# Another order of the same operations in a windowed-attention and gated-projection kernel

## The chip, the cores and the metric

The kernel runs on one core of a Trainium2 chip. The metric is the device time of one execution in microseconds; the median of three runs is given, and one further execution was profiled.

## What is computed

Batch 4, 8 heads, 768 positions, head size 64. The attention keeps, for each position, the 4 first positions ("sinks") and a window of 128 positions that ends at it. Its output is the input x of a gated projection with 512 channels.

```python
scores = scale * np.matmul(q, k.transpose(0, 1, 3, 2))
keep = is_sink | in_window
scores = np.where(keep, scores, -1000000000.0)
a = softmax(scores)                       # over the kept positions
x = (a @ v).transpose(0, 2, 1, 3).reshape(B, S, H * D)
for k in range(K):                        # K = 5, causal
    gate_pre += conv_w[k][None, None, :] * xp[:, k:k + S, :]
gate = 1.0 / (1.0 + np.exp(-gate_pre))
val = x @ w_val
return (gate * val @ w_out).astype(np.float32)
```

The weights come as 64-bit floats; the kernel turns each into a high and a low 32-bit part.

## The kernel before

The attention runs in 24 steps, one for a batch, a third of the positions (256) and half of the heads; the names below carry the step's number, as in `tx.7`. Two steps (2m and 2m+1) make one group m of 256 rows and all 512 channels for the projection; there are 12 groups. The whole program is a list of names, ORDER, which the last loop of `banded` walks through: each name calls one function, which issues its instructions there and then. An engine takes its own instructions in the order in which they were issued, and waits by semaphores for the other engines. So ORDER sets the sequence on each of the engines and on the queue that starts the DMAs (SP), and nothing else does.

The names, in the order of the work, with the lines that the profile shows:

- `kq`, `vv`: DMAs of k and q, and of v (with the sink values at the first third). `wvl`, `wol`: DMAs of a quarter of a weight.
- `wva` to `wvf`, `woa` to `wof`: decoding of a quarter of w_val or w_out. a, c, d, f are mostly ScalarE (L140, L159, L154, L186), b is VectorE on integers (L143, L145, L151), c has a GpSimd product (L160), e is four TensorE matmuls (L181 to L183). For two quarters of w_out a variant without TensorE is used, with VectorE (L151 to L168) and GpSimd (L172).
- `s0`, `s1`: scores of half a step, 32 small matmuls (L395), then VectorE masking and maximum (L400, L404 or L409). `e0`, `e1`: the exponentials, eight ScalarE instructions (L420). `rec`, `norm`: reciprocal, and GpSimd scaling (L435 to L443).
- `tx`: 16 transposes of the probabilities on TensorE (L455); `px`, `py`: copies on VectorE (L486) and ScalarE (L494). `sk`: one transpose of the sink probabilities (L463); `ts`: its copy (L471 or L473).
- `vl`: 48 or 32 matmuls with v (L513); `si`: two matmuls with the sink values (L521), which `sv` prepares (L260 on ScalarE, L263 on GpSimd).
- `xc`, `xh`, `hd`: ScalarE copies of the result (L528, L536, L540); `xl`, `c4`: GpSimd (L544, L549); `c0`, `c1`: the convolution on VectorE (L557); `th`: tanh (L562).
- `v0` to `v3`: a quarter of x @ w_val for group m, 12 matmuls of 128 by 128 on 256 columns each (L576), the last four of which read xl; `y`, `g`, `h`, `l`: copy, gate and split of the result (L582, L595, L601, L605).
- `o0` to `o3`: half of one 128-row block of the output product, six matmuls of 128 by 128 on 512 columns (L629); `t0`, `t1`: copy to an osb buffer (L648), `d0`, `d1`: its DMA.
- `fill.n`: n matmuls on zeros (L227), whose result nothing reads.

Two pairs of PSUM banks serve the scores and tx in turn, two single banks serve the projection, the output, sk and the decoding, and one pair serves vl. There are three buffers of k, q and v, four of raw weights, three of osb. Lines of the loop:

```python
    with tc.manual_schedule():
        for n in ORDER.split():
            f, args = events[n]
            f(*args)
```

Of the kernel before, what the change touches and what calls it, by code (L numbers as in the profile page):

```python
# [47 lines left out]
s0.7 l0.1 vl.4 y1.1 g1.1 e0.7 h1.1 l1.1 s1.7 s1.8 o2.1 si.4 e1.7 tx.5 xc.4 xh.4 px.5 hd.4 c4.4 c0.4 c1.4 o3.1
t1.1 o0.1 e1.8 py.5 kq.9 sk.5 ts.5 norm.6 o1.1 t0.1 tx.6 py.6 rec.7 vl.5 si.5 xc.5 xl.4 px.6 c4.5 sk.6 ts.6
hd.5 xh.5 xl.5 s0.9 s0.8 th.4 norm.7 v0.2 v1.2 e0.9 c0.5 tx.7 c1.5 e0.8 rec.8 norm.8 v2.2 py.7 px.7 g0.2 h0.2  # L50
s1.9 kq.10 s1.10 vl.6 l0.2 si.6 xc.6 c4.6 th.5 sk.7 ts.7 hd.6 d0.1 vv.7 v3.2 xh.6 sv.7 o2.2 g1.2 c0.6 o0.2
h1.2 c1.6 e1.9 rec.9 l1.2 o3.2 e1.10 d1.0 t1.2 tx.8 xl.6 px.8 py.8 vl.7 si.7 xc.7 hd.7 xh.7 sk.8 norm.9 ts.8
c4.7 s0.10 tx.9 th.6 px.9 c0.7 d1.11 c1.7 o1.2 t0.2 e0.10 rec.10 xl.7 v0.3 vv.8 py.9 v1.3 vv.9 g0.3 h0.3 kq.12
s0.12 kq.11 s0.11 th.7 d1.2 l0.3 vl.8 si.8 xc.8 hd.8 c4.8 xh.8 d0.2 s1.11 sk.9 e0.11 norm.10 ts.9 xl.8 v2.3
e1.11 v3.3 c0.8 c1.8 g1.3 e0.12 h1.3 o2.3 s1.12 l1.3 kq.13 s1.13 rec.11 e1.12 rec.12 vl.9 si.9 xc.9 th.8 c4.9
hd.9 xh.9 tx.10 px.10 kq.16 py.10 o3.3 t1.3 vv.10 norm.11 o0.3 o1.3 t0.3 c0.9 c1.9 sk.10 ts.10 s0.13 tx.11
py.11 px.11 norm.12 xl.9 vv.13 vl.10 si.10 xc.10 hd.10 xh.10 kq.14 d1.3 tx.12 py.12 px.12 c4.10 c0.10 warm_up
v0.4 xl.10 v1.4 g0.4 d1.1 h0.4 l0.4 vv.11 c1.10 th.9 v2.4 e1.13 v3.4 g1.4 sk.11 ts.11 s1.14 s0.14 h1.4 vl.11
si.11 o0.4 sk.12 ts.12 e0.13 rec.13 l1.4 xc.11 hd.11 c4.11 sv.13 e0.14 norm.13 c0.11 o1.4 kq.18 e1.14 t0.4
c1.11 kq.15 o2.4 d0.3 o3.4 s0.18 s0.15 vv.12 th.11 xh.11 sv.12 vl.12 si.12 t1.4 xc.12 tx.13 rec.14 hd.12 xl.11  # L60
v0.5 c4.12 norm.14 xh.12 e0.15 px.13 c0.12 c1.12 v2.5 xl.12 v3.5 g1.5 py.13 th.10 v1.5 g0.5 h0.5 sk.13 ts.13
s1.15 h1.5 s1.18 d0.4 e1.15 vl.13 l0.5 si.13 o0.5 l1.5 xc.13 rec.15 hd.13 xh.13 s0.16 e0.16 th.12 tx.14 px.14
o2.5 kq.17 o1.5 t0.5 py.14 c4.13 c0.13 o3.5 t1.5 vv.14 e0.18 xl.13 vv.18 c1.13 s1.16 d1.5 sk.14 ts.14 norm.15
sk.15 ts.15 sv.18 vl.14 si.14 xc.14 hd.14 tx.15 px.15 e1.16 c4.14 c0.14 rec.16 py.15 norm.16 e1.18 c1.14 xh.14
v0.6 v1.6 g0.6 v2.6 h0.6 s0.17 vv.15 kq.19 s0.19 vl.15 si.15 rec.18 l0.6 th.13 vv.16 e0.17 xc.15 v3.6 g1.6
xl.14 c4.15 s1.17 hd.15 s1.19 th.14 h1.6 sk.16 ts.16 l1.6 xh.15 c0.15 xl.15 e1.17 rec.17 kq.20 e0.19 o0.6 o1.6
t0.6 tx.16 py.16 c1.15 px.16 v0.7 v1.7 norm.18 sk.18 ts.18 s0.20 d1.4 kq.21 e1.19 d0.6 vl.16 v2.7 e0.20 g0.7
h0.7 norm.17 l0.7 si.16 xc.16 c4.16 hd.16 tx.18 px.18 py.18 tx.17 v3.7 px.17 c0.16 o2.6 o3.6 th.15 g1.7 vv.23
rec.19 xh.16 c1.16 py.17 t1.6 s1.20 h1.7 xl.16 s0.21 e1.20 sk.17 ts.17 norm.19 o0.7 vv.17 th.16 rec.20 d0.5
l1.7 vl.17 si.17 xc.17 c4.17 hd.17 xh.17 e0.21 xl.17 norm.20 d1.6 c0.17 tx.19 py.19 o2.7 o3.7 o1.7 t0.7 c1.17  # L70
th.17 px.19 t1.7 kq.23 d1.7 s1.21 vl.18 d0.7 si.18 xc.18 c4.18 hd.18 vv.19 xh.18 e1.21 sv.19 tx.20 vv.20 px.20
c0.18 v2.8 xl.18 v3.8 g1.8 h1.8 kq.22 c1.18 th.18 v0.8 v1.8 sk.19 py.20 ts.19 g0.8 h0.8 vl.19 si.19 s1.22 l1.8
rec.21 s0.22 xc.19 hd.19 l0.8 xh.19 c4.19 xl.19 sk.20 o0.8 ts.20 o1.8 c0.19 c1.19 norm.21 e1.22 t0.8 d0.8 o2.8
e0.22 rec.22 v0.9 norm.22 th.19 tx.21 px.21 py.21 vl.20 si.20 vv.21 xc.20 c4.20 hd.20 xh.20 xl.20 s1.23 e1.23
s0.23 vv.22 v1.9 g0.9 h0.9 o3.8 t1.8 v2.9 e0.23 v3.9 l0.9 c0.20 c1.20 rec.23 sk.21 norm.23 ts.21 vl.21 si.21
xc.21 c4.21 g1.9 h1.9 l1.9 tx.22 py.22 px.22 tx.23 py.23 hd.21 xh.21 o2.9 xl.21 o0.9 o3.9 c0.21 o1.9 t1.9 t0.9
# [815 lines left out]
```

## Time and profile before

| | |
|---|---|
| median of 3 runs | 263.68 us (263.66 to 263.72) |
| profiled execution | 264.63 us, span 262.8 us |
| mean granted TensorE clock | 0.997 |
| TensorE busy | 253.6 us (97%) |
| VectorE busy | 204.7 us (78%) |
| ScalarE busy | 188.7 us (72%) |
| GpSimd busy | 177.4 us (67%) |

The span runs from the first to the last instruction of the profiled execution. In the rows, PE is TensorE, PEld its weight loads, DVE VectorE, ACT ScalarE, POOL GpSimd, SP the queue of the DMAs. `L513` is line 513 of the kernel; `out<-in` are the program's names for tiles. Matmuls are pipelined, so one's duration overlaps the next; distances are read from start to start.

### The profile page before, as it was taken

Reading aid. Unit: us, or ns where it says so; the run is one execution under the profiler, and the core shown is the slowest. Engines: PE = TensorE matmul, PEld = TensorE weight load, DVE = VectorE, ACT = ScalarE, POOL = GpSimd, SP = SyncE. Lnnn points to the kernel's source line nnn. Section 1 sums busy time; section 2 is a strip of 40 time slices with the busy share of each in tenths; the row PEclk is TensorE's granted clock in tenths of the full one; section 3 lists DMA queues with packets and bytes.
Section 4 is the critical chain, followed back from the end, with each engine's and each line's share of the span. In section 5 each row is a group of like instructions: output and inputs, shape, how many; then the busy total and the mean of one; then the engine's idle time right before and its main releaser. Section 6 shows DMA issues by size and latency. Waiting matters only on the chain.

```text
span 262.8 us, 9921 instructions
## 1 busy us (share of the span) xinstructions
PE 253.6 (97%) x3960; PEld 205.5 (78%) x3964; DVE 204.7 (78%) x561; ACT 188.7 (72%) x692; POOL 177.4 (67%) x241
## 2 busy tenths in 40 slices
...
PEclk9999999999999999999999999999999999999998
...
GB/s 201 379 340 341 113 262 74 109 168 144 106 78 118 183 131 146 218 171 180 63 174 2 161 81 326 78 185 111 142 4 231 68 106 59 2 122 0 2 44 128
DMA packets 27541, 36.45 MB, mean 139 GB/s; under 512 B 2272, under 2 KB 24032, under 8 KB 27488
## 3 DMA queue, kind: packets, MB, share of 16 engines
...
q14 instruction: 20, 0.16, 0.2%
...
## 4 chain that ended last, share of the span: by engine, by line
PE 79%; ACT 9%; POOL 4%; DMA 4%; DVE 1%; issue 1%; POOLq 0%
PE ac L576 24%; PE ac L629 22%; PE xv L513 11%; PE pr L395 9%; PE pr L455 4%; ACT w L420 4%; PE pr L629 3%; PE xv L521 2%; DMA raw<-in_w_val_dram 2%; DMA vs<-in_vsk_dram 2%; POOL xl L544 1%; PE ac L463 1%; POOL gl L605 1%; POOL vh L263 1%; ACT wv_p L140 1%
## 5 line engine op out<-in xcount | busy, mean ns | idle before, releaser
L557 DVE SCALAR_TENSOR_TENSOR sg<-xv,cw,sg 128x256 f32<-128x256 f32 x192 | 77.8, 474 | 3.3 <-POOL sg L549 2.9
L435 POOL TENSOR_TENSOR wx<-w,sm 128x512 f32<-128x512 f32 x48 | 49.2, 1047 | 5.7 <-DVE sm L427 4.0
L420 ACT ACTIVATE w<-pr,ngm 128x132 f32<-128x132 f32 x136 | 48.6, 370 | 1.6
L576 PE MATMUL ac<-xh,wvh 128*128 128x256 f32 x192 | 48.7, 288 | 0.0
L605 POOL TENSOR_TENSOR gl<-sg,gh 128x512 fp32r<-128x512 f32 x24 | 30.8, 1290 | 26.0 <-ACT gh L601 25.8
L576 PE MATMUL ac<-xh,wvl 128*128 128x256 f32 x192 | 47.0, 279 | 0.0
L549 POOL TENSOR_TENSOR sg<-xt,cw 128x512 f32<-128x512 f32 x24 | 25.5, 1063 | 17.9 <-ACT xt L528 16.5
L576 PEld LDWEIGHTS ac<-xh,wvh 128*128 128x128 f32 x192 | 36.2, 189 | 1.7 <-issue 0.5
L576 PEld LDWEIGHTS ac<-xh,wvl 128*128 128x128 f32 x192 | 36.1, 188 | 0.2
L395 PE MATMUL pr<-k,q 64*32 64x168 f32 x1536 | 35.0, 307 | 0.6 <-DVE wt L486 0.2
L513 PEld LDWEIGHTS xv<-wt,v 64*64 64x64 f32 x1024 | 30.3, 133 | 6.1 <-issue 2.6
L513 PE MATMUL xv<-wt,v 64*64 64x192 f32 (+2 forms) x1024 | 34.5, 278 | 0.2 <-ACT wt L494 0.2
L544 POOL TENSOR_TENSOR xl<-xt,xh 128x512 fp32r<-128x512 f32 x24 | 31.0, 1290 | 3.9 <-DVE sm L427 2.5
L629 PE MATMUL ac<-woh,gh 128*128 128x512 f32 x80 | 33.2, 415 | 0.0
L629 PE MATMUL ac<-woh,gl 128*128 128x512 f32 x80 | 31.8, 397 | 0.3 <-POOL gl L605 0.3
L629 PE MATMUL ac<-wol,gh 128*128 128x512 f32 x80 | 31.7, 396 | 0.0
L576 PE MATMUL ac<-xl,wvh 128*128 128x256 f32 x192 | 30.4, 280 | 0.1
L395 PEld LDWEIGHTS pr<-k,q 64*32 64x32 f32 x1536 | 24.0, 106 | 8.1 <-issue 2.1
L400 DVE COPY_PREDICATED pr<-low,pr 128x256 f32<-128x256 uint8 x48 | 20.3, 422 | 9.6 <-PE pr L395 4.9
L420 ACT ACTIVATION_READ_ACCUMULATOR w<-pr,ngm 128x1 f32 x136 | 27.6, 203 | 0.0
L576 PEld LDWEIGHTS ac<-xl,wvh 128*128 128x128 f32 x192 | 25.9, 188 | 0.3 <-POOL xl L544 0.3
L404 DVE TENSOR_REDUCE ngm<-pr 128x4 f32<-128x528 f32 x34 | 24.0, 707 | 1.2
...
## 6 DMA issues: line engine op xcount, KB each, us to landing
...
q<-in_qt_dram SPq DMA_DIRECT2D x23, 256.0 KB, 4.6
out_dram<-osb SPq DMA_DIRECT2D x23, 256.0 KB, 2.5
v<-in_vt_dram SPq DMA_DIRECT2D x8, 256.0 KB, 5.0
...
```

Of the source, the lines that this page charges most:

```text
L395: nc.tensor.matmul(ss[e * QB:(e + 1) * QB, j, c * n + x0:c * n + x1], q[js, g, (4 * c + e) * QB:(4 * c + e + 1) * QB], k[js, g, (2 * c + e ...
L400: nc.vector.copy_predicated(sv[:, :, :, :D], low[:, None, None, :].to_broadcast([P, 2, 2, D]), sv[:, :, :, 2 * HB:])
L404: nc.vector.tensor_reduce(out=ngm[:, g], in_=sv[:, :, :, :PK], axis=mybir.AxisListType.X, op=ALU.max)
L420: nc.scalar.activation(out=w[:, g, j, c], in_=sx[:, j, c, :PK], func=AF.Exp, scale=0.125 if whole else -1.0, bias=ngm[:, g, j, c:c + 1], a ...
L435: nc.gpsimd.tensor_tensor(out=t[:, n].rearrange("p c h x -> p h c x"), in0=w[:, :, :, at], in1=sm.to_broadcast([P, 4, 2, D]), op=ALU.mult)
L513: nc.tensor.matmul(acc[o * D:(o + 1) * D, g, x0 + h * D:x0 + (h + a1 - a0 + 1) * D], v[js, g, n], t[js, n % 2, n // 2, g, a0:a1 + 1].rearr ...
L544: nc.gpsimd.tensor_tensor(out=half(xls, s, "xl", F32R), in0=xts[s], in1=half(xhs, s, "xh", F32R).bitcast(F32), op=ALU.subtract)
L549: nc.gpsimd.tensor_tensor(out=half(sg, s, "sg", F32), in0=xts[s], op=ALU.mult, in1=cw[:, g, KT - 1:].to_broadcast([P, 2, PQ]))
L557: nc.vector.scalar_tensor_tensor(out=g, in0=x, scalar=a, in1=g, op0=ALU.mult, op1=ALU.add)
L576: nc.tensor.matmul(acc[:, h], a[:, kc, cs], x[:, kc], start=(n == 0), stop=(n == 11))
L605: nc.gpsimd.tensor_tensor(out=gl, in0=g, in1=gh.bitcast(F32), op=ALU.subtract)
L629: nc.tensor.matmul(acc, a[:, kc, ts], x[:, kc], start=(kc + n == 0), stop=(kc + n == 5))
```

## The change

ORDER is replaced by another sequence of the same 849 names; no function changes. The first lines and some later ones of both:

```diff
--- before.py
+++ after.py
@@ -34,50 +34,50 @@
 ORDER = """
-masks load_conv wvl.0 signs kq.0 leads conv_weights fill.5 wva.0 wvb.0 wvd.0 s0.0 wvl.1 s1.0 wvc.0 wve.0 wvl.2
-wva.1 kq.1 wvb.1 e0.0 blanks wva.2 wvb.2 vv.0 e1.0 wvf.0 fill.10 s1.1 wvc.2 wvc.1 rec.0 norm.0 wvd.1 e1.1 s0.1
-fill.4 fill.7 kq.2 s1.2 wol.0 woa.0 wve.1 sv.0 e0.1 e1.2 wob.0 woc.0 wol.2 tx.0 fill.6 px.0 sk.0 py.0 rec.1
-ts.0 wod.0 s0.2 vl.0 woe.0 wvl.3 wva.3 norm.1 wvb.3 kq.3 e0.2 s0.3 wof.0 wvf.1 si.0 xc.0 tx.1 px.1 fill.6 c4.0
-kq.5 wvc.3 rec.2 norm.2 xh.0 wvd.2 hd.0 c0.0 wvd.3 e0.3 wve.2 c1.0 py.1 wol.3 wol.1 woa.1 wve.3 vv.1 wob.1
-wvf.3 sv.1 tx.2 py.2 px.2 s1.3 xl.0 sk.1 ts.1 wod.1 wvf.2 kq.4 vl.1 si.1 xc.1 c4.1 sk.2 ts.2 kq.6 hd.1 woc.1
-s0.4 xh.1 vv.2 woe.1 c0.1 e1.3 rec.3 woa.3 th.0 vv.5 e0.4 xl.1 v0.0 v1.0 c1.1 y0.0 wob.3 woa.2 norm.3 g0.0
-wod.3 h0.0 vl.2 wob.2 th.1 s1.4 e1.4 l0.0 v2.0 v3.0 woe.3 woe.2 y1.0 g1.0 vv.6 tx.3 px.3 si.2 xc.2 hd.2 wof.1
-h1.0 s0.6 o2.0 o0.0 rec.4 xh.2 py.3 c4.2 c0.2 l1.0 wof.2 s0.5 c1.2 s1.6 kq.7 wod.2 e0.6 wof.3 o1.0 t0.0 o3.0
-norm.4 sk.3 e0.5 vv.3 ts.3 t1.0 xl.2 vl.3 si.3 xh.3 xc.3 hd.3 xl.3 c4.3 sk.4 th.2 s1.5 ts.4 tx.4 sv.6 px.4
-e1.5 kq.8 c0.3 scalars d0.0 py.4 rec.5 v0.1 v1.1 y0.1 c1.3 e1.6 rec.6 v2.1 norm.5 g0.1 th.3 h0.1 v3.1 vv.4
...
-o1.10 l1.11 o1.11 t0.10 d0.10 t0.11 o3.10 t1.10 o2.11 d1.10 d0.11 o3.11 t1.11
+masks load_conv d1.11 fill.6 wvl.0 kq.0 signs leads conv_weights wva.0 wvl.2 wvb.0 s0.0 wvc.0 wvd.0 wva.2 e0.0
+s1.0 kq.1 wvb.2 wve.0 wvl.1 e1.0 fill.5 s1.1 wva.1 blanks wvb.1 wvc.2 rec.0 fill.4 norm.0 fill.6 e1.1 kq.2
+wvc.1 wvf.0 wol.0 wvl.3 s0.1 s1.2 e0.1 wvd.1 fill.10 rec.1 woa.0 tx.0 px.0 sk.0 vv.0 wve.1 e1.2 wob.0 wol.3
+s0.2 py.0 wva.3 norm.1 vl.0 kq.3 tx.1 woc.0 wod.0 ts.0 px.1 woe.0 wvb.3 vv.1 sv.0 si.0 e0.2 wvf.1 xc.0 xh.0
+vv.2 hd.0 s0.3 c4.0 rec.2 fill.7 norm.2 wvd.2 py.1 c0.0 wof.0 woa.3 c1.0 wve.2 wob.3 kq.4 sv.1 e0.3 tx.2 sk.1
+py.2 xl.0 kq.6 px.2 ts.1 woe.3 vl.1 sk.2 si.1 s1.3 s1.4 wvc.3 wol.1 ts.2 xc.1 xh.1 wvd.3 hd.1 wve.3 xl.1 wvf.2
+c4.1 woa.1 wvf.3 wob.1 v0.0 e1.3 c0.1 c1.1 wol.2 v1.0 wod.1 wof.3 woa.2 th.0 v2.0 kq.5 woc.1 v3.0 rec.3 y0.0
+vv.3 g0.0 s0.4 woe.1 wob.2 e1.4 s1.6 th.1 y1.0 e0.4 h0.0 vl.2 vv.6 wof.1 g1.0 woe.2 norm.3 vv.5 si.2 xc.2 xh.2
+s0.6 l0.0 kq.7 c4.2 wof.2 s0.5 sk.3 ts.3 h1.0 wod.2 wod.3 l1.0 o2.0 o0.0 tx.3 hd.2 sv.6 o3.0 c0.2 e0.6 px.3
+c1.2 rec.4 xl.2 norm.4 o1.0 e0.5 py.3 s1.7 e1.6 th.2 s0.7 vl.3 t0.0 si.3 d0.0 s1.5 tx.4 t1.0 xh.3 xc.3 hd.3
+vv.4 kq.8 e0.7 px.4 xl.3 sk.4 ts.4 c4.3 v0.1 d1.0 c0.3 v1.1 v2.1 rec.6 e1.5 rec.5 py.4 kq.15 c1.3 v3.1 y0.1
...
+px.5 norm.6 rec.7 xh.4 c0.4 xl.4 ts.5 py.5 o2.1 e1.8 kq.9 c1.4 s0.8 tx.6 norm.7 vl.5 si.5 t0.1 sk.6 py.6 px.6
+e0.8 xh.5 o3.1 kq.10 rec.8 ts.6 xc.5 hd.5 xl.5 scalars s1.9 t1.1 c4.5 norm.8 vv.7 s0.9 e1.9 sk.7 ts.7 c0.5
+v0.2 sv.7 th.4 v1.2 c1.5 v2.2 v3.2 tx.7 e0.9 g0.2 th.5 h0.2 py.7 tx.8 g1.2 l0.2 vl.6 h1.2 si.6 px.7 rec.9 px.8
...
+o0.11 g1.11 o1.10 h1.11 l1.11 o1.11 t0.10 o3.10 t0.11 d0.10 d0.11 o2.11 t1.10 o3.11 d1.10 t1.11
 """
 SKA = 6
```

`d1.11` stands for nothing in either list: the last block is sent by `o3.11` and `t1.11` themselves.

## Rows read from the trace of the kernel before

**Rows 1.** The page's slices: the granted TensorE clock in 40 equal slices of the span, in tenths of full speed.

```profile
PEclk9999999999999999999999999999999999999998
```

**Rows 2.** Busy time by stretches: the stretch and its length in us, then for each engine its busy us and (x instructions), the granted clock, the DMA share and GB/s.

```profile
30.00:40.00 10.00, 8.72 (x139) 6.03 (x138) 9.74 (x23) 9.94 (x36) 9.30 (x12) 1.00 0.57 178
40.00:50.00 10.00, 10.00 (x174) 8.62 (x173) 9.82 (x19) 9.04 (x32) 6.20 (x8) 1.00 0.38 114
50.00:60.00 10.00, 10.00 (x190) 7.68 (x190) 8.06 (x31) 8.29 (x33) 8.68 (x11) 1.00 0.51 137
...
38.20:200.00 161.80, 161.67 (x2787) 136.44 (x2786) 137.02 (x383) 126.11 (x485) 117.35 (x152) 1.00 0.44 134
```

**Rows 3.** TensorE's instructions in order of time, from five places of the trace: start us, duration us, engine, line, operation, out<-in, shape, count.

```profile
46.31 0.71 PE L455 MATMUL pr<-ident,wx 64*128 64x64 f32 x16
46.83 0.36 PE L521 MATMUL xv<-skt,vh 64*128 64x256 f32 x2
...
87.09 0.38 PE L521 MATMUL xv<-skt,vh 64*128 64x256 f32 x2
87.41 0.33 PE L463 MATMUL ac<-ident,skb 128*128 128x128 f32 x1
87.49 0.36 PE L576 MATMUL ac<-xh,wvh 128*128 128x256 f32 x1
...
95.63 0.80 PE L395 MATMUL pr<-k,q 64*32 64x168 f32 x32
96.36 0.71 PE L455 MATMUL pr<-ident,wx 64*128 64x64 f32 x16
...
190.22 0.39 PE L521 MATMUL xv<-skt,vh 64*128 64x256 f32 x2
190.45 0.66 PE L455 MATMUL pr<-ident,wx 64*128 64x64 f32 x16
191.03 0.50 PE L629 MATMUL ac<-woh,gh 128*128 128x512 f32 x1
...
203.82 0.27 PE L463 MATMUL ac<-ident,skb 128*128 128x128 f32 x1
204.03 1.21 PE L513 MATMUL xv<-wt,v 64*64 64x192 f32 x32
```

**Rows 4.** The same view for the first 40 us; in brackets the idle time before an instruction and what ended it.

```profile
10.45 0.50 PE L183 MATMUL ac<-wv_f,plus 128*128 128x512 f32 x1 [0.85 <-POOL wv_f L160]
...
13.06 1.37 PE L395 MATMUL pr<-k,q 64*32 64x168 f32 x64
14.36 2.55 PE L227 MATMUL ac<-zero 128*128 128x512 bf16 x10
...
17.57 1.13 PE L181 MATMUL ac<-wv_t,ident 128*128 128x512 f32 x2
...
19.09 0.71 PE L455 MATMUL pr<-ident,wx 64*128 64x64 f32 x16
...
38.21 0.28 PE L576 MATMUL ac<-xh,wvh 128*128 128x256 f32 x1
```

**Rows 5.** The chain of work that ended last, in order of time: start us, us that the piece adds to the chain (overlap with the next taken off), what.

```profile
19.70 1.52 ACT w L420 x8
...
22.87 0.52 ACT woh L154
...
27.06 0.55 ACT wv_p L159
...
31.48 0.57 ACT wo_p L140
32.05 0.49 ACT wvl L186
...
58.85 5.80 PE ac L576 x48
```

**Rows 6.** ScalarE's instructions in order of time, the copy xh.1.

```profile
36.27 0.68 ACT L536 ACTIVATE xh<-xv 128x512 fp32r<-128x512 f32 x1
```

**Rows 7.** TensorE's instructions in order of time at v0.2 and v1.2, and at o0.8.

```profile
80.05 1.03 PE L576 MATMUL ac<-xl,wvh 128*128 128x256 f32 x4
...
81.85 0.62 PE L576 MATMUL ac<-xl,wvh 128*128 128x256 f32 x4
...
207.36 0.40 PE L629 MATMUL ac<-wol,gh 128*128 128x512 f32 x1
208.04 0.50 PE L629 MATMUL ac<-woh,gl 128*128 128x512 f32 x1 [0.28 <-POOL gl L605]
```

**Rows 8.** Groups of instructions by line over the whole span: line, engine, operation, out<-in, shapes, count | busy us, mean ns of one | idle us before them and what ended it.

```profile
L544 POOL TENSOR_TENSOR xl<-xt,xh 128x512 fp32r<-128x512 f32 x24 | 31.0, 1290 | 3.9 <-DVE sm L427 2.5 <-ACT xt L528 1.2
...
L528 ACT ACTIVATE xt<-xv 128x512 f32<-128x512 f32 x24 | 14.4, 600 | 10.8 <-PE xv L521 10.8
```

**Rows 9.** All instructions of line 143: count, then duration in ns as minimum, median and maximum, first and last start us.

```profile
L143 DVE TENSOR_SCALAR wv_t<-wv_p x4: 420/518/814, 6.7 to 24.7; 128x512 int32<-128x512 int32 x4
L143 DVE TENSOR_SCALAR wo_t<-wo_p x4: 427/530/967, 18.8 to 42.7; 128x512 int32<-128x512 int32 x4
```

**Rows 10.** The same for line 227, the matmuls on zeros.

```profile
L227 PE MATMUL ac<-zero x34: 379/379/634, 3.7 to 27.6; 128*128 128x512 bf16 x34
```

**Rows 11.** DMA issues of one kind: queue, count, KB each, median us from issue to landing.

```profile
out_dram<-osb SPq DMA_DIRECT2D x23, 256.0 KB, 2.5
```

More of the change, by code (lines that the diff above doesn't have):

```diff
@@ L47 @@
-e1.5 kq.8 c0.3 scalars d0.0 py.4 rec.5 v0.1 v1.1 y0.1 c1.3 e1.6 rec.6 v2.1 norm.5 g0.1 th.3 h0.1 v3.1 vv.4
[L48 to L76, printed above, removed]
@@ L77 @@
-c1.21 px.23 th.20 sk.22 ts.22 vl.22 si.22 xc.22 c4.22 xh.22 xl.22 sk.23 ts.23 d1.9 hd.22 c0.22 c1.22 v0.10
-v2.10 v1.10 th.22 g0.10 v3.10 h0.10 l0.10 vl.23 si.23 xc.23 c4.23 hd.23 xh.23 xl.23 th.21 flag g1.10 o0.10
-o2.10 d1.8 c0.23 c1.23 v0.11 v1.11 th.23 g0.11 h0.11 l0.11 v2.11 d0.9 v3.11 g1.11 o0.11 h1.10 l1.10 h1.11
-o1.10 l1.11 o1.11 t0.10 d0.10 t0.11 o3.10 t1.10 o2.11 d1.10 d0.11 o3.11 t1.11
+masks load_conv d1.11 fill.6 wvl.0 kq.0 signs leads conv_weights wva.0 wvl.2 wvb.0 s0.0 wvc.0 wvd.0 wva.2 e0.0
@@ new lines @@
+e1.7 vl.4 th.3 y1.1 g0.1 h0.1 norm.5 g1.1 s1.8 h1.1 tx.5 si.4 xc.4 hd.4 l0.1 sk.5 vv.8 l1.1 c4.4 o0.1 o1.1
+px.5 norm.6 rec.7 xh.4 c0.4 xl.4 ts.5 py.5 o2.1 e1.8 kq.9 c1.4 s0.8 tx.6 norm.7 vl.5 si.5 t0.1 sk.6 py.6 px.6
+e0.8 xh.5 o3.1 kq.10 rec.8 ts.6 xc.5 hd.5 xl.5 scalars s1.9 t1.1 c4.5 norm.8 vv.7 s0.9 e1.9 sk.7 ts.7 c0.5
+v0.2 sv.7 th.4 v1.2 c1.5 v2.2 v3.2 tx.7 e0.9 g0.2 th.5 h0.2 py.7 tx.8 g1.2 l0.2 vl.6 h1.2 si.6 px.7 rec.9 px.8
+xc.6 kq.12 xh.6 s1.10 l1.2 py.8 c4.6 o0.2 norm.9 hd.6 vv.12 c0.6 e1.10 s0.10 o2.2 o3.2 c1.6 e0.10 s0.12 vl.7
@@ new lines @@
+d0.1 si.7 tx.9 rec.10 t1.2 xc.7 xh.7 xl.6 c4.7 px.9 hd.7 e0.12 xl.7 s1.12 o1.2 t0.2 e1.12 py.9 c0.7 kq.11 c1.7
+th.6 v0.3 sk.8 th.7 ts.8 v1.3 g0.3 norm.10 s1.11 h0.3 s0.11 l0.3 d1.2 vl.8 si.8 sk.9 xc.8 hd.8 v2.3 xh.8 c4.8
+ts.9 e1.11 o0.3 c0.8 c1.8 kq.13 vv.9 v3.3 g1.3 xl.8 s0.13 e0.11 h1.3 th.8 s1.13 vl.9 tx.10 si.9 xc.9 sk.10
+ts.10 l1.3 rec.11 o1.3 xh.9 kq.18 hd.9 c4.9 e0.13 px.10 e1.13 c0.9 d1.1 vv.10 c1.9 o2.3 o3.3 norm.11 py.10
+s0.18 s1.18 vl.10 tx.11 rec.12 t0.3 si.10 sk.11 t1.3 xl.9 ts.11 hd.10 v2.4 py.11 xc.10 xh.10 d1.3 th.9 c4.10
@@ new lines @@
+norm.12 v0.4 px.11 kq.14 c0.10 v3.4 v1.4 vv.11 vv.13 c1.10 g0.4 sv.12 tx.12 g1.4 vl.11 e0.18 si.11 py.12 px.12
+d0.3 h0.4 s0.14 h1.4 s1.14 xc.11 l0.4 hd.11 d0.2 vv.14 sk.12 l1.4 o2.4 ts.12 rec.13 e1.14 c4.11 o3.4 o0.4
+c0.11 e0.14 c1.11 o1.4 norm.13 tx.13 xh.11 kq.19 px.13 rec.14 t1.4 t0.4 py.13 kq.16 vl.12 si.12 xl.10 s1.15
+xc.12 s0.15 xl.11 th.10 hd.12 sk.13 c4.12 ts.13 vv.16 v2.5 sv.13 xh.12 v3.5 c0.12 th.11 g1.5 e1.15 norm.14
+e0.15 e1.18 v0.5 tx.14 c1.12 h1.5 sk.14 v1.5 px.14 l1.5 py.14 g0.5 vl.13 h0.5 ts.14 si.13 l0.5 hd.13 rec.15
```

17 lines of the change are left out of this document (added).

## The prediction, made before the changed kernel was run

> **What bounds the kernel now.** I read the slices of the page first, then the busy time by stretches, then TensorE's instructions in order of time, then ScalarE's through the first 40 us. The granted clock stands at full speed in every slice but the last [rows 1]. From 40 us on TensorE is busy in whole stretches, while the other engines leave room [rows 2]. So behind 40 us the time is the sum of TensorE's blocks, and an order can change it in two ways only: by what a block costs behind its neighbour, and by waits. In front of 40 us it is different: ScalarE is busy 9.94 of 10 us, TensorE only 8.72 [rows 2], and part of that is work on zeros. There the order of ScalarE's queue sets when the first projection, v0.0, can start: it starts at 38.21 us [rows 4].
>
> **What a block costs depends on its neighbour.** Read the distances from start to start in [rows 3]. The sink transpose (sk, L463) takes 0.08 us (87.41 to 87.49) ahead of a 128-by-128 matmul, but 0.21 us (203.82 to 204.03) ahead of the small attention matmuls of L513. The sink product (si, L521) takes 0.32 us ahead of anything (87.09 to 87.41) but a probability transpose (tx, L455): there it is 0.23 (190.22 to 190.45). A tx takes 0.58 ahead of a wide matmul (190.45 to 191.03), 0.52 ahead of si (46.31 to 46.83).
>
> **The change part by part.** Every name of the old order is in the new one, as often: 849 names, 38 zero matmuls, the same DMAs. So nothing is removed or added; the sum has three terms.
>
> *Neighbours.* Counted in the two lists, with every name that issues no matmul left out:
>
> - sk stands ahead of val or out 8 times now and 19 times then; ahead of scores, values, si, decode 15 and 5 times (once ahead of another sk before). At 0.08 and 0.21 that is 8 x 0.08 + 15 x 0.21 + 0.17 (an estimate for the one between the two) = 3.96 against 19 x 0.08 + 5 x 0.21 = 2.57: -1.4 us. At the dearest price, 0.25, which I get if scores behind it cost more than values, -1.9.
> - si ahead of tx 10 and 2 times: eight lose 0.09 each, +0.7 us.
> - tx ahead of si or another tx 3 and 12 times. At 0.52 and 0.58 to 0.60 that is -0.5 to -0.7 us; for tx ahead of sk (4 times, none before) I have no row and take the wide price. tx ahead of tx has no row here either; I price it as tx ahead of si. I take -0.6; the ends are 0 (the saving belongs to what stands ahead of tx) and -1.0.
> - val and out stand ahead of attention blocks 23 and 27 times. A score block of 32 ends 0.73 behind its start (95.63 to 96.36), 0.65 each when two follow each other (13.06 to 14.36) [rows 3, 4], so a change of shape costs about 0.1: +0.2 us at most 0.4.
>
> Sum: -1.4 + 0.7 - 0.6 + 0.2 = -1.1 us, ends -0.3 and -1.9.
>
> The Trainium skill, "TensorE: Matmul & The Clock Gate", section "Back-to-back issue gap", gives the distance of two matmuls from the columns alone, with no term for the neighbour; by it this term would be 0. The rows of sk, 0.08 against 0.21 for the same instruction, disagree with it; the case is a rival below.
>
> *The start.* Ahead of xh.1, the ScalarE copy that closes the first group's input, the new queue no longer holds wvd.3, woa.1, wvf.3, wod.1, wvf.2, woc.1; it holds woa.3 in addition. By the net steps of the chain, L154 0.52, L140 0.57, L186 0.49, L159 0.55 [rows 5], that is 2 x 0.52 + 0.57 + 2 x 0.49 + 0.55 - 0.57 = 2.6 us less. xh.1 ended at 36.95 [rows 6], so it would end near 34.4. Two things eat some of it. sv.0 on GpSimd now stands behind woc.0, so si.0, and with it ScalarE's xc.0, comes some 0.4 us later (one L160 against sv's pieces, an estimate from the engine order); behind xc.0 wait xh.0 and wvd.2, and for that wve.2. And wvd.3 now follows xh.1 (+0.5) and wve.3, the last decode ahead of v0.0, needs it for its last two matmul groups: half of the 1.52 us that an undisturbed decode takes (17.57 to 19.09 [rows 4]) plus a little, 0.9. So v0.0 starts near 34.4 + 0.4 + 0.5 + 0.9 = 36.2 instead of 38.2: 2.0 us earlier. But TensorE work was moved behind it: s0.4 (0.73) and woe.1 (1.52) now follow v0.0, s1.4 (0.57 as the second of two scores) precedes it: 1.7 us. Net -0.3 us. Bounds: -1.2 (GpSimd holds nothing up) and +0.8 (the DVE queue, which now has wob.3 and woe.3 ahead of s1.3, comes last).
>
> DMAs: kq.1 now goes out ahead of wvl.1, vv.0 behind wol.0 and wvl.3 on SP's queue. ScalarE reaches wva.1 after e1.0, and vl.0 stands behind 16 us of TensorE work, so I cost both at nothing; what covers them is ScalarE's backlog. If vv.0 came last, vl.0 would wait, at most the length of one 512 KB load. The sends (d) move as well: there are three osb buffers, and t1.5 now needs d0.5 to have landed, which stands some 3 us of TensorE work ahead of it; a send lands 2.5 us behind its issue [rows 11]. Covered, but barely; without that cover ScalarE would stand still for a few tenths, with py and exps behind it.
>
> *Waits behind 40 us.* Two of the old order's waits are large enough to see [rows 7]: the four xl matmuls of v0.2 take 1.03 us instead of 0.62 (0.4), and the third matmul of o0.8 starts 0.68 behind the second instead of 0.23 (0.45, for gl on GpSimd). In the new list the TensorE work between si.5 and v0.2 is doubled (two val blocks' worth instead of one), and between the val blocks of group 8 and o0.8 it grows by some 1 us, so both should go: -0.85. One comes: between si.3 and v0.1 only s1.5, tx.4 and sk.4 are left, 1.3 us, and the xl matmuls come some 0.9 later (eight matmuls); against this stand two copies of 0.60 and one xl of 1.29 [rows 8]: +0.3, by which all of TensorE's queue behind v0.1 moves. I take -0.3, not -0.55, since a new order has waits that a count doesn't show; ends -0.85 and +1.5.
>
> *VectorE's integer operations.* L143 takes 0.42 us at best and up to 0.81 and 0.97 [rows 9]. All eight at the minimum would give VectorE about 1 us (medians 0.52 and 0.53, two far above). In the start ScalarE is the full engine, so I cost it at nothing; ends -0.4 and +0.4, since the new list moves these instructions among as much GpSimd work.
>
> The end: the last six blocks, from o0.11 to o3.11, stand in the same sequence in both lists, so the tail stays.
>
> Sum: -1.1 - 0.3 - 0.3 = -1.7 us. The profiled execution took 264.63 us (262.8 of it span), the median of the runs is 263.68; I carry the difference over: span near 261.1, profiled execution 262.9, median **262.0 us**. For this kernel 0.2% (0.53 us) is what a measurement can tell from no change.
>
> **Rivals.**
>
> *A. The neighbours' prices don't add up.* If a saved gap is only moved into the next block, the first term is about 0 and 0.6 us are left: 263.1. For it: tx's price differs by what stands ahead of it. Against: sk's two prices. This is also the case in which the change doesn't do what its words say: the clock is at full speed already, and VectorE is not what the start waits for. Chance 0.20.
>
> *B. ScalarE becomes the bound from v0.0 to v0.1 (slower).* In the old order this stretch holds 4 exps and 25 other ScalarE entries, in the new one 7 and 27. At 1.52 us an exp [rows 5] that is 4.6 us, with the two others 5.6, on top of the 17.3 us ScalarE was busy between 40 and 60 us [rows 2]: 22.9. TensorE gains s0.4, woe.1, s0.7 and s1.7 and loses s1.4, about 2.7 us on the 20.6 us from 38.21 to 58.85 [rows 4, 5]: 23.3. So ScalarE has 0.4 us to spare; if it also waits as long as before (2.7 us in those 20), v0.1 comes 2.3 us late and nothing behind it has idle time to give it back: 263.68 - 1.7 + 2.3 = 264.3. It decides once the lateness exceeds 2.2 us. Against: part of that work (e0.7, ts.4) isn't needed for v0.1. Chance 0.13.
>
> *C. TensorE's clock drops in the start (slower).* The new order opens with fill.6 instead of fill.5, and later has fill.5, then fill.4 and fill.6, then fill.10 where the old one had fill.10 early. A zero matmul takes 0.63 us while the clock is low and 0.38 when it is not [rows 10]. If waits between fill.5 and fill.10 let it fall to 1.2 GHz for some 5 us of TensorE work that nothing covers, that is +2.5 to +3: 264.7. The Trainium skill, "TensorE: Matmul & The Clock Gate", section "HAM oscillation — how this bites in real kernels", says that waiting TensorE falls back to half clock and starts the next work cold; it speaks against thinner cover. The trace agrees only in that the clock held through waits of 0.85 us [rows 4]. Chance 0.05.
>
> *D. Both engine queues fit better than counted.* The start gives its -1.2 and the waits their -0.85: 263.68 - 1.1 - 1.2 - 0.85 = 260.5. Chance 0.12.
>
> **How the numbers follow.** The forecast's own case (261.3 to 262.9) has 0.50, A 0.20, D 0.12, B 0.13, C 0.05. Faster by over 0.2% (below 263.15): the forecast, D and a third of A, 0.68. Within: the rest of A and a little of B, 0.17. Slower: the rest of B, and C, 0.15. The range runs from D to between A and B's far side: 260.4 to 264.3; the likeliest case alone 261.3 to 262.9.
>
> **What would show it.** v0.0 starting near 36.2 us; sk mostly 0.08 us from its successor; TensorE's busy sum near 252; no 1.03 us xl group at v0.2; the granted clock full in all slices but the last. Wrong if v0.1 starts more than 1 us later than 59.0 us with ScalarE full before it, if idle time of TensorE behind 40 us grows beyond 2 us, or if a slice of the first ten shows a lower clock.

## The result: 1.4% slower, and where the time went

The changed kernel takes **267.27 us** (median of four runs, 267.25 to 267.32) against 263.70 for the kernel before in the same session (263.66 to 263.76): ratio 1.0136, 95% interval 1.0118 to 1.0153. The forecast was 262.0, the range ended at 264.3; both are wrong, and so is the sign. The profiled execution of the new kernel took 267.28 us, its span 265.5.

The page of the new kernel, TensorE's and the other engines' busy time and the slices of the granted clock:

```profile
PE 253.2 (95%) x3961; PEld 204.8 (77%) x3964; DVE 210.2 (79%) x561; ACT 188.1 (71%) x692; POOL 177.8 (67%) x241
PEclk9999999999999999999999999999999999999999
```

The clock is full in every slice (a 9 stands for 90% or more; the mean granted clock is 1.000), so rival C is out. TensorE is busy about as long as before (253.6 us there). The busy time that moved most is VectorE's: 204.7 us before, 210.2 now, for the same 561 instructions. The stretches that answer to [rows 2]:

```profile
30.00:40.00 10.00, 9.27 (x147) 6.91 (x146) 9.90 (x17) 8.06 (x27) 9.60 (x12) 1.00 0.37 104
40.00:50.00 10.00, 8.66 (x176) 6.47 (x175) 9.72 (x23) 9.52 (x37) 6.11 (x8) 1.00 0.13 43
50.00:60.00 10.00, 8.68 (x121) 5.96 (x121) 9.90 (x30) 8.04 (x31) 7.30 (x7) 1.00 0.35 109
```

From 40 to 60 us TensorE is no longer busy throughout (8.66 and 8.68 of 10), ScalarE has some room (9.52 and 8.04), and VectorE (the third pair) is close to full in all three stretches. TensorE's instructions at the two places that the prediction named, v0.0 and v0.1, and below them v0.1 before:

```profile
37.23 0.28 PE L576 MATMUL ac<-xh,wvh 128*128 128x256 f32 x1
...
64.38 0.36 PE L576 MATMUL ac<-xh,wvh 128*128 128x256 f32 x1
```

```profile
58.78 0.39 PE L576 MATMUL ac<-xh,wvh 128*128 128x256 f32 x1
```

v0.0 comes 1.0 us earlier than before [rows 4], v0.1 5.6 us later. To split this into work and waiting I gave each block of TensorE's list the start-to-start distance that its kind has ahead of its successor's kind in the trace of before, and summed these down each list. What a block starts later than that sum is waiting, counted from the start of the span:

| | sum of blocks | waited by v0.0 | by v0.1 | by the last block |
|---|---|---|---|---|
| before | 243.80 | 8.04 | 8.59 | 12.88 |
| after | 242.61 | 8.72 | 13.15 | 16.59 |

So the neighbours gave 1.19 us, the start lost 0.68, the stretch from v0.0 to v0.1 lost 3.9 (4.44 against 0.55), and behind v0.1 the new order gained 0.85 (3.44 against 4.29): together +2.5, for spans that differ by 2.7. How the total splits hangs on the distance that stands for a pair. With the least, the lower quarter or the median of each pair the stretch loses 3.9 to 4.1 us and the start 0.7 to 0.9; the neighbours give 1.2 to 2.2, and the part behind v0.1 gains 0.3 to 0.9. The loss in the stretch is firm, the two gains are less so.

**What holds that stretch.** The shares of the engines in the whole chain of work that ended last, before and then now:

```profile
PE 79%; ACT 9%; POOL 4%; DMA 4%; DVE 1%; issue 1%; POOLq 0%
```

```profile
PE 79%; DVE 15%; issue 2%; POOL 1%; ACT 1%; DVEq 0%; POOLq 0%
```

VectorE had 1% of it and has 15%. Pieces of the new chain, in order of time, from 34 us to v0.1 (start, us that the piece adds, what):

```profile
34.94 0.77 DVE wo_e L151
35.71 1.43 DVE wo_f L166
37.16 1.66 DVE wo_p L168
...
47.46 1.12 DVE wo_t L143
...
51.66 1.19 DVE wo_e L151
...
64.62 1.41 PE ac L576 x12
```

VectorE's integer operations are not more, they are longer. Instructions of their lines in the new kernel (count, ns as minimum, median, maximum, first and last start):

```profile
L143 DVE TENSOR_SCALAR wo_t<-wo_p x4: 416/792/1189, 20.8 to 47.4; 128x512 int32<-128x512 int32 x4
...
L145 DVE SCALAR_TENSOR_TENSOR wv_t<-wv_p,wv_t x4: 691/693/1641, 6.8 to 27.0; 128x512 int32<-128x512 int32 x4
L145 DVE SCALAR_TENSOR_TENSOR wo_t<-wo_p,wo_t x4: 693/760/1412, 22.0 to 48.6; 128x512 int32<-128x512 int32 x4
...
L166 DVE TENSOR_SCALAR wo_f<-raw x2: 419/957/1495, 35.6 to 52.8; 128x512 int32<-128x512 int32 x2
...
L168 DVE SCALAR_TENSOR_TENSOR wo_p<-raw,wo_f x2: 695/1180/1664, 37.2 to 53.2; 128x512 f32<-128x512 uint32 x2
```

The same view of before, for L145 and L166:

```profile
L145 DVE SCALAR_TENSOR_TENSOR wv_t<-wv_p,wv_t x4: 691/692/693, 7.1 to 25.5; 128x512 int32<-128x512 int32 x4
L145 DVE SCALAR_TENSOR_TENSOR wo_t<-wo_p,wo_t x4: 691/692/693, 19.5 to 43.3; 128x512 int32<-128x512 int32 x4
...
L166 DVE TENSOR_SCALAR wo_f<-raw x2: 415/418/420, 45.3 to 46.7; 128x512 int32<-128x512 int32 x2
```

Over all 28 of these instructions (L143, L145, L151, L166, L168 of eight decodes), what they take above their lines' minima is 6.9 us now and 1.6 before; the difference, 5.3, is nearly all of VectorE's growth of 5.5. And what they meet shows in the order of time, VectorE first, then GpSimd:

```profile
35.63 1.50 DVE L166 TENSOR_SCALAR wo_f<-raw 128x512 int32<-128x512 int32 x1
37.16 1.66 DVE L168 SCALAR_TENSOR_TENSOR wo_p<-raw,wo_f 128x512 f32<-128x512 uint32 x1
...
35.37 1.47 POOL L160 TENSOR_TENSOR wv_f<-wv_e,wv_p 128x512 fp32r<-128x512 f32 x1
36.80 1.48 POOL L544 TENSOR_TENSOR xl<-xt,xh 128x512 fp32r<-128x512 f32 x1
38.23 1.50 POOL L549 TENSOR_TENSOR sg<-xt,cw 128x512 f32<-128x512 f32 x1
```

L166 starts inside L160 and ends 0.29 us behind it; L168 starts inside L544 and ends 0.5 behind that. GpSimd pays too: L160 takes 1.47 where it took 1.28 before, L549 1.50 where its median is 1.05. By the trace, 11 of the 28 now overlap a GpSimd instruction of 0.9 us or more for over 0.05 us (called a meeting here), and carry 6.5 of the 6.9 us; before it was 5 with 1.1. So the new order has more of these meetings than the old one, not as many.

How they reach TensorE shows in what ended the idle time before an instruction (in brackets), first TensorE, then ScalarE:

```profile
25.24 1.13 PE L181 MATMUL ac<-wo_t,ident 128*128 128x512 f32 x2 [1.00 <-ACT skt L471]
...
44.99 1.12 PE L181 MATMUL ac<-wo_t,ident 128*128 128x512 f32 x2 [1.23 <-ACT vc L582]
...
39.94 0.20 ACT L417 ACTIVATE ngm<-ngm 128x4 f32<-128x4 f32 x1 [1.91 <-DVE ngm L404]
```

These are the two longest waits of TensorE between 14 us and v0.1; no wait of TensorE names a DMA. The engines in the brackets are ScalarE, but ScalarE itself had stood still for VectorE: 0.82 us for the L145 at 22.0 us, which with the L143 ahead of it took 1.5 us more than their minima, and 1.91 us for the L404 that came behind the L166 and L168 above.

### The profile page after: what moved, and what is told of

It is laid out like the page before. It is cut to its first block, busy times and chain, and to the rows that moved or that the text cites. A ratio compares the mean times of both kernels' runs of the same rounds, so it can differ in the third digit from the quotient of the medians.

```text
span 265.5 us, 9964 instructions
## 1 busy us (share of the span) xinstructions
PE 253.2 (95%) x3961; PEld 204.8 (77%) x3964; DVE 210.2 (79%) x561; ACT 188.1 (71%) x692; POOL 177.8 (67%) x241
## 4 chain that ended last, share of the span: by engine, by line
PE 79%; DVE 15%; issue 2%; POOL 1%; ACT 1%; DVEq 0%; POOLq 0%
PE ac L576 24%; PE ac L629 20%; PE xv L513 10%; PE pr L395 9%; PE pr L455 5%; DVE sg L557 3%; PE pr L629 3%; PE xv L521 2%; PE ac L463 2%; DVE sx L409 2%; DVE pr L400 1%; PE ac L227 1%; PE ac L181 1%; DVE wo_t L143 1%; DVE wt L486 1%
## 5 line engine op out<-in xcount | busy, mean ns | idle before, releaser
L557 DVE SCALAR_TENSOR_TENSOR sg<-xv,cw,sg 128x256 f32<-128x256 f32 x192 | 77.7, 474 | 10.2 <-POOL sg L549 7.0
L549 POOL TENSOR_TENSOR sg<-xt,cw 128x512 f32<-128x512 f32 x24 | 26.0, 1084 | 23.6 <-ACT xt L528 23.4
L576 PEld LDWEIGHTS ac<-xh,wvl 128*128 128x128 f32 x192 | 36.2, 188 | 0.3
L544 POOL TENSOR_TENSOR xl<-xt,xh 128x512 fp32r<-128x512 f32 x24 | 31.1, 1300 | 5.9 <-ACT xh L536 5.4
L404 DVE TENSOR_REDUCE ngm<-pr 128x4 f32<-128x528 f32 x34 | 24.1, 708 | 1.2
```

The source lines that it names most:

```text
L404: nc.vector.tensor_reduce(out=ngm[:, g], in_=sv[:, :, :, :PK], axis=mybir.AxisListType.X, op=ALU.max)
L544: nc.gpsimd.tensor_tensor(out=half(xls, s, "xl", F32R), in0=xts[s], in1=half(xhs, s, "xh", F32R).bitcast(F32), op=ALU.subtract)
L549: nc.gpsimd.tensor_tensor(out=half(sg, s, "sg", F32), in0=xts[s], op=ALU.mult, in1=cw[:, g, KT - 1:].to_broadcast([P, 2, PQ]))
L557: nc.vector.scalar_tensor_tensor(out=g, in0=x, scalar=a, in1=g, op0=ALU.mult, op1=ALU.add)
L576: nc.tensor.matmul(acc[:, h], a[:, kc, cs], x[:, kc], start=(n == 0), stop=(n == 11))
```

## The experiments

Theory 1: the new order loses 4 us because in its start VectorE's decode instructions and GpSimd's long ones hold each other up, and it gains behind v0.1 as forecast. Rivals: the sequence of VectorE's queue itself (more of other work ahead of what TensorE needs), waits of the new order in general, and gaps that don't add up. The kernel before stood at 263.97 us beside the first four kernels, 263.99 beside the second four, 263.80 and 264.21 beside the last two pairs. With the waiting counted as above:

| kernel | us | sum of blocks | by v0.0 | by v0.1 | by the last block |
|---|---|---|---|---|---|
| e3_new_plain | 264.49 | 242.61 | 7.87 | 10.32 | 13.76 |
| e4_old_plain | 265.77 | 243.80 | 8.36 | 10.10 | 14.11 |
| e7_new_two | 265.17 | 242.61 | 7.33 | 10.95 | 14.38 |
| e8_new_one | 266.92 | 242.61 | 9.36 | 13.14 | 16.53 |
| e5_old_start_cut | 263.78 | 242.75 | 7.55 | 9.12 | 12.67 |
| e11_old_to_64 | 263.46 | 242.85 | 8.01 | 8.57 | 12.86 |

**The meeting taken away, in both orders.**

```diff
-        nc.vector.tensor_scalar(out=t, in0=p, scalar1=3, op0=ALU.logical_shift_left, ...)
-        nc.vector.scalar_tensor_tensor(out=t, in0=p, scalar=-2147483648, in1=t, ...)
+        plain(tf, pf)
+        plain(tf, pf)
...
+    def plain(o, x):
+        nc.vector.tensor_reduce(out=o, in_=x[..., None], axis=mybir.AxisListType.X, op=ALU.max)
```

> The new order, with the five integer instructions of each weight decode on VectorE (L143, L145, L151, L166, L168) replaced by reductions over an axis of length one: same tiles, same count, one SBUF input, about 0.6 us each by the nearest row; the weights' low parts are therefore not the real ones. Theory 1 (what VectorE lost it lost because these instructions and GpSimd's hold each other up): each takes its 0.6 us however GpSimd stands, v0.1 starts 2 us or more earlier than 64.4, and the time is 263 to 265 us, at most 1 us above the same edit on the old order. Rival (it is the sequence of VectorE's queue itself, more decode work ahead of the scores' and the convolution's entries): 266.5 us or more, 3 us above the same edit on the old order.

> The same replacement in the old order (the weights' low parts are not the real ones). Theory 1 and its rival alike: VectorE was not what the old start waited for, so 263.2 to 264.4 us; it is the base against which the new order with this edit is read.

Measured: 264.49 us for the new order (ratio to before 1.0021, 1.0009 to 1.0032), 265.77 for the old (1.0065, 1.0044 to 1.0087). With the same edit the new order is 1.3 us *faster* than the old, where the unedited one is 3.6 slower. The first expectation held. The second missed: the old order pays 1.8 us for the edit, by which eighteen of its 28 instructions became 0.26 us longer, so VectorE did stand in the old start's way. The replaced instructions of the new order (line 143 is here the reduction):

```profile
L143 DVE TENSOR_REDUCE wv_t<-wv_p x8: 674/686/686, 6.3 to 25.9; 128x512 f32<-128x512 f32 x8
...
L143 DVE TENSOR_REDUCE wo_t<-wo_p x8: 674/686/687, 20.5 to 45.7; 128x512 f32<-128x512 f32 x8
L143 DVE TENSOR_REDUCE wv_e<-wv_t x4: 686/686/687, 7.7 to 26.7; 128x512 f32<-128x512 f32 x4
```

None of them is held (0.67 to 0.69 us), at the same places in the same queue among the same GpSimd work, though 16 of the 28 meet an instruction of it. TensorE's two waits of 1.00 and 1.23 us are gone, and v0.0 starts at 36.39 us. Waiting by v0.1 is 10.32 us against 10.10 in the old order: of the 4.6 us by which the new order was behind there, 0.2 are left. In the stretch from v0.0 to v0.1 alone it is 0.7 of 3.9, and the start makes up the rest; one VectorE instruction that the edit leaves alone, L595, is still held there, 1.66 us against 0.96 in the old order. The rival, the sequence of VectorE's queue, would have kept its 3 us; it falls.

**One form at a time, in the new order.**

```diff
 # e7: L145 and L168 (two SBUF tiles), L145 below      e8: L143, L151 and L166 (one SBUF tile), likewise
-        nc.vector.scalar_tensor_tensor(out=t, in0=p, scalar=-2147483648, in1=t, ...)
+        nc.vector.tensor_reduce(out=tf, in_=pf[..., None], axis=mybir.AxisListType.X, op=ALU.max)
```

> The new order, with only the two decode instructions that read two SBUF tiles (L145, L168) replaced by a reduction over an axis of length one, 0.68 us each, as long as the two undisturbed (0.69); the weights' low parts are not the real ones. L143, L151, L166 stay. If both forms are held by GpSimd: the ten replaced ones lose their 2.8 us of lengthening and the eighteen others keep about their 4.0, so 265.5 to 266.7 us. If only the pairs of the two reading two tiles matter: 264.5 or less. If this form doesn't matter: 267 or more.

> The new order, with only the decode instructions that read one SBUF tile (L143, L151, L166; 0.42 us undisturbed) replaced by the same reduction at 0.68 us; the weights' low parts are not the real ones. L145 and L168 stay. VectorE gets eighteen times 0.26 us more to do (4.7) and loses the 4.0 us by which these are lengthened: if both forms are held, 266 to 267.3 us, and the traces show L145 and L168 between 0.69 and 1.7 us, the reductions all near 0.68. If the one-input form is not held by GpSimd but only queued, the time grows by the added work, to 268.5 or more.

Measured: 265.17 us (1.0049, 1.0034 to 1.0065) and 266.92 (1.0115, 1.0096 to 1.0134). The first lies 0.3 below the range expected for "both forms are held" and 0.7 above the one for "only the pairs of the two", the second inside the range for "both". What stayed is held in either, first the one-input form of the first kernel, then the two-input form of the second:

```profile
L143 DVE TENSOR_SCALAR wo_t<-wo_p x4: 414/1092/1190, 20.0 to 45.3; 128x512 int32<-128x512 int32 x4
...
L166 DVE TENSOR_SCALAR wo_f<-raw x2: 414/960/1507, 34.0 to 50.7; 128x512 int32<-128x512 int32 x2
```

```profile
L145 DVE SCALAR_TENSOR_TENSOR wv_t<-wv_p,wv_t x4: 693/695/1396, 7.4 to 27.0; 128x512 int32<-128x512 int32 x4
...
L168 DVE SCALAR_TENSOR_TENSOR wo_p<-raw,wo_f x2: 692/1222/1751, 36.9 to 53.2; 128x512 f32<-128x512 uint32 x2
```

**The orders spliced at v0.1.**

```diff
 # e1: old list up to py.4 rec.5, then what is left in the new list's sequence:
 py.4 rec.5 d1.11 s1.7 e1.6 s0.7 vv.4 e0.7 v0.1 d1.0 v1.1 v2.1 rec.6 ...
 # e2: new list up to v0.1, then what is left in the old list's sequence
 e1.5 c0.3 scalars py.4 rec.5 v0.1 v1.1 y0.1 c1.3 rec.6 v2.1 norm.5 ...
```

> The old order up to the first val block of the second group (v0.1), and from there the remaining names in the new order's sequence. Theory 1 (the loss arises ahead of v0.1, where VectorE's decode instructions are held by GpSimd's; behind v0.1 the new order gains): v0.1 starts near 58.8 us as in the old order, the part behind it is about 1.7 us shorter (the neighbours' share behind v0.1, some 0.9, and the waits at v0.2 and o0.8, 0.85), so about 261.5 to 262.3 us. Rival (the new order as a whole makes waits that the old one had not, and they only show early): 263.5 us or more.

> The new order up to v0.1, then the remaining names in the old order's sequence. Theory 1: v0.1 starts near 64.4 us as in the new order, behind it the old order's neighbours and waits come back, so 1 to 2 us slower than the new order: 268.3 to 269.3 us. Rival: the time lost ahead of v0.1 is given back by slack behind it, 266 us or less.

Measured: 266.72 us (1.0114, 1.0082 to 1.0145) and 270.10 (1.0231, 1.0206 to 1.0255). The second went as theory 1 says and 0.8 us beyond its range: v0.1 at 64.29 us, nothing given back behind it; why it is so much stays open. The first missed and lies where the rival had it, by its seam: two score blocks that the old list issues behind v0.1 stand ahead of it in a bunch, and TensorE waited 2.7 us for the exps. Busy time of that splice around the seam:

```profile
58.00:62.00 4.00, 1.33 (x46) 1.02 (x50) 3.97 (x9) 3.97 (x20) 3.17 (x4) 0.85 0.98 339
62.00:66.00 4.00, 4.00 (x66) 3.31 (x51) 2.80 (x19) 2.35 (x13) 2.79 (x5) 0.72 0.05 16
```

After TensorE was busy 1.33 of 4 us the granted clock falls: 0.85 and 0.72 are means over time at 2.4 and at 1.2 GHz. v0.1, at 63.51 us, runs into it. That price belongs to the splice, so the run says nothing of the new order's second part.

**Better seams.**

```diff
 # e5: old list up to xl.2, then the rest in the new list's sequence:
 sk.3 e0.5 vv.3 ts.3 t1.0 xl.2 d1.11 sv.6 s1.7 e1.6 th.2 s0.7 vl.3 si.3 d0.0 s1.5 tx.4 ...
 # e9: as e5, but
 t1.0 xl.2 d1.11 sv.6 vl.3 si.3 s1.7 e1.6 th.2 s0.7 d0.0 s1.5 tx.4 ...
 # e11: old list up to xc.4 without o2.1, then the rest in the new list's sequence:
 s1.7 s1.8 si.4 e1.7 tx.5 xc.4 d1.11 d1.0 kq.15 hd.4 sk.5 vv.8 c4.4 o0.1 o1.1 ... py.5 o2.1 ...
 # e12: as e11, but o2.1 stays in its old place and ts.5 stands behind sk.5
```

> The old order up to xl.2 (two val and four out blocks of the first group issued), and from there the remaining names in the new order's sequence: a place where the two lists have issued the same names but for four that use no TensorE. The first splice, at v0.1, had put tx.4, s1.7 and s0.7 in one bunch ahead of v0.1, where TensorE stood 2.7 us for the exps. Theory 1 (the loss is the start's): v0.1 starts between 58.5 and 59.8 us, from there the new order's growth of some 3.4 us of waits against the old one's 4.3, and fewer dear neighbours: about 261.8 to 262.8 us, below both kernels. Rival (the new order's part behind the first group waits by itself): 263.7 us or more.

> The second splice (old order up to xl.2, then the new one), with s1.7, e1.6, th.2 and s0.7 moved behind vl.3 and si.3: TensorE has 1.8 us of work (vl.3 and si.3) in front of the place where it stood 0.96 us for the exps. Theory 1: the wait goes and nothing takes its place, so 0.6 to 1.0 us below the second splice's 263.8, and the first kernel faster than both: 262.7 to 263.2 us. Rival (ScalarE and VectorE are full up to v0.1, the wait moves to the next block that needs them): 263.5 us or more.

> A third splice, at a place where no TensorE block is bunched: the old order up to xc.4 (about 64 us, both val groups issued), then the remaining names in the new order's sequence, o2.1 where the new order has it. Theory 1 (the new order loses only ahead of v0.1 and gains behind it): v0.1 starts as in the old order, 58.2 to 58.8 us; behind it the neighbours give 1.0 us and the two waits at v0.2 and o0.8 0.85: 262.0 to 262.8 us, faster than both kernels. Rival (the first kernel's start leaves the engines in a state that the new order's continuation pays for, as at the two earlier seams): 263.4 us or more.

> The same splice, but o2.1 stays where the old order has it and ts.5 is put directly behind sk.5, so that o0.1 gets its bank. One val or out block stands ahead of v0.2's group earlier, but o0.1 waits for ts.5 on ScalarE. Theory 1: within 0.5 us of the third splice, at most that much slower, 262.2 to 263.2 us. Rival: 263.4 us or more.

Measured: e5 263.78 us (0.9992, 0.9983 to 1.0001), e9 264.19 (1.0027, 1.0008 to 1.0047), e11 263.46 (0.9973, 0.9959 to 0.9987), e12 263.58 (0.9975, 0.9962 to 0.9989). All four miss theory 1's ranges, by 1.0, 1.0, 0.7 and 0.4 us, and lie where their rivals had them. Each has a wait at the same kind of place, the seam (e12 one of 0.7 us, for ts.5). TensorE in e5, and then in e11 (idle time and what ended it in brackets):

```profile
55.79 0.51 PE L395 MATMUL pr<-k,q 64*32 64x168 f32 x15 [0.89 <-ACT w L420]
```

```profile
69.32 0.71 PE L455 MATMUL pr<-ident,wx 64*128 64x64 f32 x16 [0.87 <-DVE ngm L409]
```

Apart from that the numbers of e11 in the table are what was expected: v0.1 starts at 58.75 us, the blocks sum to 0.96 us less than in the old order, and the waiting by the last block is the old order's (12.86 and 12.88), with this one wait in it. e9 moved e5's wait from ScalarE to VectorE (s1.5 and tx.4 stood 1.1 and 0.7 us for ngm), as its rival said; in its profiled execution the clock then falls, as in e1, and its median holds runs with and without that. So, less its one wait, e11 has the gain behind v0.1, and the join gives most of it back; that is a subtraction, no run here shows the time without a join. e11 and e12, 0.27% and 0.25% below the kernel before and not to be told apart, are the fastest kernels here.

**The neighbours' price by itself.**

```diff
 # e6, old order: seven pairs moved, as
-sk.6 ts.6 hd.5 xh.5 xl.5 s0.9 s0.8 th.4 norm.7 v0.2
+hd.5 xh.5 xl.5 s0.9 s0.8 th.4 norm.7 sk.6 ts.6 v0.2
 # e10, on e5: nine sinks moved one block to the front, as
-si.9 xc.9 sk.10
+sk.10 si.9 xc.9
```

> The old order with seven pairs sk.s ts.s moved to stand directly ahead of a val block (sk.4 ahead of v0.1, sk.6 v0.2, sk.8 v0.3, sk.11 v0.4, sk.13 v0.5, sk.15 v0.6, sk.19 v2.8), nothing else. Theory of the prediction's first term (a sink transpose costs 0.08 us ahead of a 128-by-128 matmul, 0.21 ahead of an attention matmul): 7 times 0.13, so 0.9 us less, 262.5 to 263.1. Rival (the gap is only moved into the next block): 263.5 to 263.9, no difference.

> The second splice with nine sink transposes behind v0.1 (sk.5, 7, 9, 10, 11, 12, 13, 17, 20) moved one TensorE block to the front, so that an attention block stands behind them and not a val or out block; nothing else moves. The prediction's first term (0.08 us ahead of a 128-by-128 matmul, 0.21 ahead of an attention matmul): 9 times 0.12 to 0.13, so 1.1 us more, 1.7 with the dearer tx ahead of sk in five places: 264.8 to 265.6 us. Rival (the gaps don't add up): 263.6 to 264.0.

Measured: e6 270.73 us (1.0249, 1.0224 to 1.0274), far outside both expectations. Its blocks sum to 0.5 us less, but its waiting by the last block is 19.62 us. TensorE's longest wait of it, by line (us in total, times, longest):

```profile
PE ac L576 <- DVE skt L473: 3.6, 3, 2.0
```

A sink transpose takes one of the two accumulator banks until its ts copy is out; moved directly ahead of a val group it takes the bank that the group needs. These three waits are 3.6 of the 6.7 us by which its waiting grew; the rest is not told apart here, and the granted clock fell as well (0.94 between 150 and 180 us). So e6 says nothing of the price, only that the position of a cheap block is bound by what holds its bank.

e10 measured 266.30 us (1.0090, 1.0075 to 1.0106), 2.5 above e5. The gaps add up, and they are larger than I said (0.7 us above the expected range). Around sk.10 in e5:

```profile
113.04 0.71 PE L455 MATMUL pr<-ident,wx 64*128 64x64 f32 x16
113.56 0.36 PE L521 MATMUL xv<-skt,vh 64*128 64x256 f32 x2
113.86 0.33 PE L463 MATMUL ac<-ident,skb 128*128 128x128 f32 x1
113.94 0.48 PE L629 MATMUL ac<-woh,gh 128*128 128x512 f32 x1
```

and in e10:

```profile
113.73 0.71 PE L455 MATMUL pr<-ident,wx 64*128 64x64 f32 x16
114.38 0.33 PE L463 MATMUL ac<-ident,skb 128*128 128x128 f32 x1
114.63 0.38 PE L521 MATMUL xv<-skt,vh 64*128 64x256 f32 x2
114.95 0.50 PE L629 MATMUL ac<-woh,gh 128*128 128x512 f32 x1
```

The same three blocks take 0.90 us from tx to out in the one sequence, 1.22 in the other: sk 0.25 instead of 0.08, and tx ahead of it 0.65 instead of 0.52. Over all nine places, with the block behind each included, the difference is 0.20 to 0.36 us, 2.8 in all, close to the 2.5 measured. Rival A falls.

## Why the prediction was wrong, by its own steps

1. *Neighbours, -1.1.* Right in sign and cause: -1.19 by the prices above, and e3 against e4, where little else differs, is 1.3 us. That the size fits so closely is partly luck: by other readings of the same distances it is -1.2 to -2.2, and e10 has the single prices dearer than the sum took them. The sign named for it, a busy sum near 252 us, did not come (253.2); why is not shown. The distance that the Trainium skill gives by the columns ("TensorE: Matmul & The Clock Gate", "Back-to-back issue gap") would have made this step 0; e10 shows 0.08 and 0.25 for one instruction by its successor.
2. *The start, -0.3.* Wrong sign, inside its bounds: +0.7. v0.0 came at 37.23, not 36.2. The bound that I named had VectorE's queue come last, and it did, though not at the entries that I named: TensorE's wait of 1.00 us at 25.24 hangs on the held L143 and L145. Where these are not held, in e3, v0.0 starts at 36.39.
3. *Waits behind 40 us, -0.3.* The two that should go went: the four xl matmuls of v0.2 take 0.63 us (1.03 in [rows 7]), and TensorE's waits no longer name gl; behind v0.1 the new order waits 0.85 us less, as the step had it. The one that should come, +0.3 ahead of v0.1, came as +3.9. That is the failed sum. It is also the sign of being wrong that did come: TensorE stands idle 2.66 us between 40 and 60 us alone.
4. *VectorE's integer operations, 0 with ends of 0.4.* **This is the step that failed**, in three ways. It was costed at nothing because "in the start ScalarE is the full engine"; but [rows 2] show VectorE at 9.74 and 9.82 of 10 us between 30 and 50 us, fuller than ScalarE in the second stretch. The cover did not exist. A price was in [rows 9], 0.97 against 0.42 us, 0.55 for the dearest meeting; I read the spread as time to be won (1.4 us over the eight, not the "about 1" that I took from the medians) and did not look at what ran on GpSimd then. And the number of meetings, 5 before, was never counted in the new list ("as much GpSimd work" stood for a count). The runs show 11 meetings in its place, and VectorE 5.3 us longer. At 0.55 us each, six more meetings are 3.3 us, an estimate: a meeting cost 0.2 us on average in the old trace and 0.6 in the new one. So a price was there to be read in the old trace; whether the count could have been foretold, by laying the queues of both engines beside each other, is not shown.
5. *The carry-over, +0.95.* The forecast kept the profiled execution of before 0.95 us above its median. The new kernel's lies at its median (267.28 and 267.27). So 0.9 of the miss is base, not change. Part of it can be the start: profiled executions of other unedited kernels with the old start have v0.0 anywhere from 37.72 (e5) to 38.19 us (e11), before has 38.21, at the late end. Where the rest of the 0.95 lies stays open.

Rival B was right in its place (v0.0 to v0.1) and its sign, wrong in its engine and its size: VectorE, not ScalarE (which stood still 1.91 us for it), and 3.9 us, not 2.3. The sign "v0.1 more than 1 us later with ScalarE full before it" would have missed it by naming the engine.

With the miss of 5.3 us put together: 3.6 in the stretch ahead of v0.1, 1.0 in the start, 0.9 in the base, less 0.2 that the other steps came out better.
